# Block sums of v for four head pairs made from the window rows, and unread products in TensorE's first idle time

## The chip, the core and the metric

The kernel runs on one NeuronCore of a Trainium2 chip. The metric is the device time of one execution in microseconds, as a median over runs. Of the engines, the text uses TensorE (PE in the profile; its weight loads are PEld), VectorE (DVE), ScalarE (ACT), GpSimd (POOL), and SyncE (SP), which only issues transfers here. Transfers are issued by SP (queue q1) and POOL (queue q0) and carried by 16 DMA engines.

## What is computed

The program is an attention layer followed by two layers of experts. Cut to what matters:

```
# attention: 2 batches x 8 heads, 768 rows, 64 columns; blocks of 32, window 16
k_sum = k.reshape(B, H, 24, 32, D).max(axis=3)
v_sum = v.reshape(B, H, 24, 32, D).mean(axis=3)
scores = concat(where(|i - j| < 16, q k^T / 8, -1e9), q k_sum^T / 8 + log(32))
attn   = softmax(scores) @ concat(v, v_sum)
# layer 1: 4 experts, out += p[:, e] * (relu(x @ w1[e]) @ w2[e])
# layer 2: 8 experts, the same, with p from a softmax gate and 8 rounds of row and column scaling
```

## The kernel before

**Attention.** The 16 heads are worked in 8 pairs, 0 to 7 (`pairs`). A pair's queries are cut into 12 tiles of 64 rows. Such a tile sees 96 rows of k and v (its own 64 and 16 on either side) and the 24 block sums, so a tile has 120 columns (`KX`: 96 window columns, `KW`, and 24 block columns, `NS`). For a pair the kernel does the following.

- `add_loads`: SP loads k (L1048), q (L1055), all 768 rows of v with six following rows to a partition (`vn`, L1062, 384 KB), and once more the rows of v by windows: `vs` holds, for each of the 12 tiles, its 96 rows (L1074, four transfers).
- `add_keys`, `add_queries`: TensorE transposes k and q (L1094, L1156). ACT and DVE copy them to `kw` and `bd`, DVE takes the maxima of the key blocks (L1123), and L1137 spreads these to every tile's last 24 columns.
- `add_values`: DVE adds neighbouring rows of `vn` (L241, `rows`), three products with the selector `sel` then give the 24 block means (L1196, `sums`), DVE copies them out (L1203), and SP writes them to every tile of `vs` (L1208). For a pair in `VROWS` the addition is left out and six products are made.
- `add_group`, three times for each pair: scores of four tiles (L1226 for the mask, L1232), the row maximum (L1248), exponentials (L1254), sums (L1260), POOL's multiplication (L1269), transposes (L1278), products with `vs` (L1293), and the copy to the layer's input (L1304).

`kn`, `qn`, `vn`, `vs`, `kw` and `bd` exist twice, so pair i + 2 overwrites what pair i used.

**Experts.** Each of the 96 steps (48 units of 256 hidden columns, 2 halves of the rows) multiplies by a scheme with seven products instead of eight, each in three parts (high and low halves). The products with w1 are L306 and those with w2 are L629. Weights are loaded by SP (L479), and then split by ACT (L486, L499) with sums made by POOL's transfers (L502, L515). The first layer-1 steps need the first four pairs, so their products are interleaved with the last pairs' attention.

**Order.** Nothing is ordered at run time. Every operation is recorded by `op(engine, span, reads, writes, due, ...)`, and `run_work` lists them by a model: `SPAN` holds durations, `due` the wanted times, and ties go to the earlier due time. What it lists is each engine's fixed order. Constants such as `AHEAD` (how early a pair's loads are due), `WAIT0` (behind which pair's key load the first weights may be loaded), `XDUE`, `TURN`, `SOONER` and `FINAL` move due times. `take_of` gives a product the PSUM bank that the model has free first.

Of the kernel before, what the change touches and what calls it, by code (L numbers as in the profile page):

```python
# [12 lines left out]
ALU = mybir.AluOpType  # L13
# [5 lines left out]
def local_global_attention_moe_moe(  # L19
# [13 lines left out]
    nc = tc.nc  # L33
    P = 128
# [5 lines left out]
    NS = S // BLOCK  # L40
# [119 lines left out]
    def view_vs(t):  # L160
# [21 lines left out]
    ks = [accs[1][:, 2 * NB_ + i * NS:2 * NB_ + (i + 1) * NS] for i in range(2)]  # L182
    vbs = [accs[1][0:KX, 2 * NB_ + (i + 1) * P:2 * NB_ + (i + 2) * P] for i in range(2)]
    maskr = place.tile([QT + 1, 6 * KX], F32R, name="maskr", tag="xc", bufs=1).rearrange(
        "x (n k) -> x n k", k=KX
# [133 lines left out]
    def relu(S, out, src, th, neg=False):  # L319
# [26 lines left out]
        "p256": (0.75, 0.77), "p512": (1.4, 1.42), "p768": (1.9, 1.93), "p384": (1.05, 1.08), "psm": (0.98, 1.02), "pks": (0.8, 0.85),  # L346
        "pid": (0.55, 0.6), "p1": (0.2, 0.25), "pmask": (3.0, 3.1), "psel": (0.9, 0.95),
        "add1": (0.95, 1.3, ADD, LAND), "add2": (0.950001, 1.3, 1.8 * ADD, LAND),
# [622 lines left out]
    def take_of(i):  # L971
        return {"of": WIDE if i < NARROW else SIDE, "left": 0, "at": 0.0, "bank": None}

    def add_setup():
        d = -20.0

        def pool(span, key, fn):
            op("POOL", span, (), [key], d, fn)
# [60 lines left out]
        vop(mask_cast, ["mask"], ["maskr"], d, "vmk", True)  # L1039

    def add_loads(i, d):
        b, hp = pairs[i]
# [9 lines left out]
        for j in range(2):  # L1052
# [6 lines left out]
            )  # L1059
        op(  # L1060
            "SP", "ldv", (), [("vn", p)], d + 0.3,
            lambda: nc.sync.dma_start(  # L1062
                out=vn, in_=v[b, 2 * hp:2 * hp + 2].rearrange("h (p c) d -> p h c d", c=VC)
            ),
        )
        t = vs[i % 2]
# [110 lines left out]
    def add_values(i, d):  # L1177
        p = i % 2
        tk = take_of(i)

        def rows():
            e = nc.gpsimd if i in VPOOL else nc.vector
            vn = vns[p]
            vadd(vn[:, :, 0::2, :], vn[:, :, 0::2, :], vn[:, :, 1::2, :], e)

        by = 1 if i in VROWS else 2
        if by == 2:
            op(
                *(("POOL", "p384") if i in VPOOL else ("DVE", "v")),
                [("vn", p)], [("vn", p)], d - 0.01, rows, True,  # L1190
            )

        def sums():
            pv = full[tk["bank"]]
            for c in range(0, VC, by):
                nc.tensor.matmul(  # L1196
                    pv[KW:KX, 0:P], sel[:, c // 2, :], vns[p][:, :, c, :],
                    start=c == 0, stop=c == VC - by,
                )

        op("PE", "pv" if by == 2 else "pv6", [("vn", p), "sel"], [("pv", i)], d, sums, take=tk)
# [180 lines left out]
    def set_places():  # L1382
# [16 lines left out]
        old1 = [("vb", 0), ("vb", 1), ("ks", 0, 0), ("ks", 0, 1), ("ks", 1, 0), ("ks", 1, 1)]  # L1399
        old1 += [("vs", 1, j) for j in range(3)] + [("bd", 1, 0), ("bd", 1, 1)]  # L1400
        for c in range(KH):
# [8 lines left out]
    SECOND = {0: "1256437", 1: "1254637"}  # L1410
    FINAL = "1567432"
    HOP, GOFF, DCOFF, LEAD, LEAD2 = 1.15, 0.15, 6.6, 1.0, 0.95
    LOPOOL = ()
    VPOOL = ()
    VROWS = (3,)
    AHEAD = 5.5
    BYPOOL = ()
    ALONG = 5.7
    NARROW = 4
    WAIT0 = 1  # L1420
    KSPOOL = (3,)
    XDUE = [-2.1, -2.5, -0.9, 0.9]
    W0DUE = -5.2
    FIRST0 = -1.1
    XPOOL = [(B11, B22), (B11, N1, B21, T3, N4), (N1, B21, B22), (N4,)]
    LATER = {-2: -0.2, 1: -0.4, 2: 0.6, 3: 0.4, 8: 0.4}
    SOONER = {-2: 0.6, -1: -0.2, 1: -0.2, 2: 0.2, 3: 0.2, 7: -0.2}
    TURN = 2.3
    M2ACT = True
    TURNPOOL = ()  # L1430
    LOX = ((0, 2, S1), (2, 2, S4), (4, 1, S1), (4, 1, S4), (15, 2, S1), (16, 1, S1), (19, 1, S4), (20, 1, S4), (20, 2, S4),)
    M2X = (6, 7, 8)
    LODVE = ((1, S1), (1, S4), (2, S1),)
    with tc.manual_schedule():
# [17 lines left out]
        for i in range(len(pairs)):  # L1452
# [5 lines left out]
            for g in range(NG):  # L1458
                add_group(i, g, A0 + (3 * i + g) * AD)
            if i == 1:  # L1460
                add_rows_first(A0 + 6 * AD)
# [87 lines left out]
```

## Time and profile before

| | us |
|---|---|
| median of 3 runs | 1539.32 (1538.97 to 1540.72) |
| profiled execution | 1539.71 |
| its span, first to last instruction | 1537.9 |
| PE busy, 9036 matmul records | 1507.3 (98%) |
| DVE, ACT, POOL busy | 1372.3, 1131.3, 485.4 |
| mean granted TensorE clock | 0.997 |

The profiled execution is 0.4 us above the median of the runs, and 1.8 us longer than its span. A matmul record covers its whole passage through the pipeline, so records overlap and a busy PE isn't PE at its peak: 12 following products of 384 columns take 2.09 us, while the mean record is 336 ns long.

### The profile page before, as it was taken

The numbers are of one execution on the slowest core, as the hardware profiler recorded it, in microseconds if no ns is written. First come the engines' busy times: TensorE is split into PE (matmuls) and PEld (weight loads), VectorE is DVE, ScalarE is ACT, GpSimd is POOL, SyncE is SP. The second block draws the span as 40 slices with busy tenths as digits, with TensorE's granted clock in tenths as the row PEclk, the third lists the DMA queues.
The fourth block names the chain that finished last, engine by engine and source line by source line (L and its number), as shares of the span: only waits on it lengthen the run. The fifth ranks groups of instructions, "written<-read, shape, count | busy, mean of one in ns | idle before, by whom it ended". The sixth has DMA issues, their size and how long they took to land.

```text
span 1537.9 us, 26663 instructions
## 1 busy us (share of the span) xinstructions
PE 1507.3 (98%) x9036; PEld 1482.9 (96%) x9036; DVE 1372.3 (89%) x2840; ACT 1131.3 (74%) x2460; POOL 485.4 (32%) x512
## 2 busy tenths in 40 slices
PE   7889999999999999999999999999999999999998
PEld 6779999999999988999999999999999999999997
DVE  7887989999988998999899899899989989989988
ACT  5888777767767779777677777777777767767765
POOL 3543233333232342343332332233332232232220
PEclk9999999999999999999999999999999999999999
DMA  9967567676666685587666666666667667667642
GB/s 218 219 121 141 114 134 132 119 134 120 124 128 125 123 149 95 106 166 151 121 119 133 123 121 132 116 126 129 124 118 136 124 112 137 124 112 137 122 71 90
DMA packets 199881, 197.83 MB, mean 129 GB/s; under 512 B 46512, under 2 KB 157760, under 8 KB 199744
## 3 DMA queue, kind: packets, MB, share of 16 engines
q0 software_dynamic: 83792, 117.73, 48.5%
q1 hardware_dynamic: 115952, 78.39, 18.5%
q8 instruction: 71, 1.16, 0.3%
q14 instruction: 66, 0.54, 0.1%
HBM read 73.97 MB, written 3.22 MB: 50 GB/s over the span
## 4 chain that ended last, share of the span: by engine, by line
PE 91%; DVE 5%; ACT 2%; DMA 1%; POOL 1%; issue 1%; SPq 0%; POOLq 0%; ACTq 0%; DVEq 0%
PE bank L306 44%; PE bank L629 43%; PE bank L1232 1%; DVE acc L241 1%; PE bank L1293 1%; DVE hoph L463 0%; ACT s L1254 0%; DMA w2lo<-raw 0%; PE bank L1196 0%; PE bank L1278 0%; DVE acc L244 0%; DVE acc L1123 0%; DMA quads<-in_k_dram 0%; DVE sm L1260 0%; ACT w2hi L486 0%
## 5 line engine op out<-in xcount | busy, mean ns | idle before, releaser
L629 PE MATMUL bank<-hoph,w2hi 128*128 128x384 f32 x2688 | 687.4, 336 | 4.7 <-ACT acc L640 1.7
L629 PEld LDWEIGHTS bank<-hoph,w2hi 128*128 128x128 f32 x2688 | 484.1, 188 | 10.9 <-ACT bank L640 4.3
L629 PE MATMUL bank<-hoph,w2lo 128*128 128x384 f32 x1344 | 449.3, 334 | 0.1
L468 ACT ACTIVATE hoph<-quads 128x384 fp32r<-128x384 f32 x672 | 335.9, 521 | 100.6 <-PE bank L629 69.0
L241 DVE TENSOR_TENSOR acc<-bank,acc 128x384 f32<-128x384 f32 x726 | 380.9, 550 | 5.6 <-PE bank L629 2.6
L306 PE MATMUL bank<-xhi,w1hi 128*128 128x384 f32 x1008 | 339.2, 336 | 1.4 <-ACT w1hi L486 1.0
L306 PE MATMUL bank<-xlo,w1hi 128*128 128x384 f32 x1008 | 337.7, 335 | 0.0
L306 PE MATMUL bank<-xhi,w1lo 128*128 128x384 f32 x1008 | 337.4, 335 | 0.1
L463 DVE TENSOR_TENSOR hoph<-quads,hoph 128x384 fp32r<-128x384 f32 x583 | 310.3, 550 | 26.2 <-ACT hoph L468 22.3
L515 POOL DMA_DIRECT2D raw<-raw x195 | 205.3, 1067 | 383.1 <-DMA raw<-raw 173.8
L640 ACT COPY bank<-bank 128x384 f32<-128x384 f32 x384 | 181.3, 472 | 115.4 <-PE bank L629 108.9
L629 PEld LDWEIGHTS bank<-hoph,w2lo 128*128 128x128 f32 x1344 | 252.3, 188 | 0.4 <-DMA w2lo<-raw 0.4
L306 PEld LDWEIGHTS bank<-xhi,w1hi 128*128 128x128 f32 x1008 | 189.4, 188 | 3.5 <-ACT w1hi L486 1.2
L306 PEld LDWEIGHTS bank<-xhi,w1lo 128*128 128x128 f32 x1008 | 189.5, 188 | 0.7 <-DVE w1lo L244 0.7
L306 PEld LDWEIGHTS bank<-xlo,w1hi 128*128 128x128 f32 x1008 | 189.4, 188 | 0.0
L640 ACT COPY acc<-bank 128x384 f32<-128x384 f32 x222 | 105.7, 480 | 84.5 <-PE bank L629 80.1
L515 POOL DMA_DIRECT2D xf<-xf x93 | 98.6, 1060 | 180.9 <-DMA xf<-xf 77.7
L323 DVE SCALAR_TENSOR_TENSOR quads<-bank,pb 128x384 f32<-128x384 f32 x178 | 98.6, 554 | 42.1 <-PE bank L306 39.2
L502 POOL DMA_DIRECT2D w2lo<-raw x65 | 68.7, 1056 | 146.6 <-ACT w2lo L499 126.6
L599 DVE SCALAR_TENSOR_TENSOR quads<-quads 128x384 f32<-128x384 f32 x192 | 105.9, 552 | 1.7
L244 DVE TENSOR_TENSOR quads<-quads 128x384 f32<-128x384 f32 x185 | 102.3, 553 | 2.7 <-ACT quads L321 0.4
L540 ACT ACTIVATE quads<-bank 128x384 f32<-128x384 f32 x192 | 91.7, 486 | 13.0 <-PE bank L306 10.2
(193 smaller groups left out, 1888.0 us busy)
## 6 DMA issues: line engine op xcount, KB each, us to landing
raw<-raw POOLq DMA_DIRECT2D x130, 256.0 KB, 4.2
raw<-in_moe_w_dram SPq DMA_DIRECT2D x66, 256.0 KB, 3.8
raw<-in_moe_w_dram SPq DMA_DIRECT2D x128, 128.0 KB, 3.0
xf<-xf POOLq DMA_DIRECT2D x62, 256.0 KB, 4.0
w2lo<-raw POOLq DMA_DIRECT2D x33, 384.0 KB, 4.8
w1lo<-raw POOLq DMA_DIRECT2D x32, 384.0 KB, 4.2
pb<-prow SPq DMA_DIRECT2D x24, 384.0 KB, 4.5
raw<-raw POOLq DMA_DIRECT2D x65, 128.0 KB, 2.7
```

The costliest lines, as they stand in the source:

```text
L241: (eng or nc.vector).tensor_tensor(out=out, in0=x, in1=y, op=ALU.add)
L244: (eng or nc.vector).tensor_tensor(out=out, in0=x, in1=y, op=ALU.subtract)
L306: nc.tensor.matmul(pm, l[:, s, cs_], x_of(b, c, r, x), start=first and i == 0, stop=i == n - 1, skip_group_check=True,)
L323: nc.vector.scalar_tensor_tensor(out=out, in0=src, scalar=0.0, in1=PB[S[1]][:, th * HB:(th + 1) * HB], op0=ALU.min if neg else ALU.max, op ...
L463: e.tensor_tensor(out=out, in0=src, in1=hi.bitcast(F32), op=ALU.subtract)
L468: aop(lambda: nc.scalar.mul(to(0), src, -1.0 if neg else 1.0), reads, writes, due, "ah")
L502: lambda: nc.gpsimd.dma_start(out=l, in_=src, accum_op=ALU.add),
L515: lambda o=o, x=x: nc.gpsimd.dma_start(out=o, in_=x, accum_op=ALU.add),
L540: aop(lambda: nc.scalar.mul(out, src, by), [kin], [kout], due)
L599: nc.vector.scalar_tensor_tensor(out=q[o], in0=q[x], scalar=-1.0, in1=q[y], op0=ALU.mult, op1=ALU.subtract)
L629: nc.tensor.matmul(cut[bank], l[:, s, cols], hop_of(t, r), start=start and i == 0, stop=i == 2, skip_group_check=True,)
L640: aop(lambda: nc.scalar.copy(out=out, in_=src), [kin], [kout], due)
```

## The change

For pairs 0 to 3 (`VWIN`) the load of `vn` and the addition of its rows are gone. The block means come from the window rows in `vs`: tile t holds 96 rows, of which each row of v is counted once by a selector that is cut to the tile, so 12 products (one for each tile) take the place of three (six for pair 3). POOL makes the selector `selw` at the start, in ten instructions. `add_idle` records 42 products of the identity with its first 64 columns, into banks that nobody reads: 12 as soon as the identity is there, 30 once pair 0's second query transpose is done. Constants that move due times are changed as well, among them `WAIT0` (1 to 5), `AHEAD`, `XDUE`, `TURN`, `SOONER`, `FINAL`; pairs 2 and 6 have their block maxima spread by POOL (`KSPOOL`) and pair 6 makes six products in place of the addition (`VROWS`). `VPOOL = (6,)` has no effect, since pair 6 has no addition.

```diff
+    W0_ = 2 * NS - 2
+    selw = accs[1][0:KW, 2 * NB_ + 3 * P:2 * NB_ + 3 * P + W0_ + 2 * NS]
+    SELW = ((NS - 2, WIN), (W0_, 0), (W0_ + 2 * NS - 2, BLOCK))
...
+        def window_sels():
+            nc.gpsimd.memset(selw, 0.0)
+            for col, row in SELW:
+                t = selw[:, col:col + 2]
+                nc.gpsimd.memset(t, 1.0 / BLOCK)
+                for sgn, base in ((1, -row), (-1, row + BLOCK - 1)):
+                    nc.gpsimd.affine_select(
+                        out=t, in_=t, pattern=[[-sgn * BLOCK, 2]], compare_op=ALU.is_ge,
+                        fill=0.0, base=base, channel_multiplier=sgn,
+                    )
...
+    def add_idle(n, span, reads):
+        for _ in range(n):
+            tk = take_of(0)
+
+            def fn(tk=tk):
+                nc.tensor.matmul(
+                    full[tk["bank"]][:, 0:D], ident, ident[:, 0:D], start=True, stop=True
+                )
+
+            op("PE", span, ["ident"] + reads, [], 1e3, fn, take=tk, use=tk)
...
+        if i not in VWIN:
+            op(
+                "SP", "ldv", (), [("vn", p)], d + 0.3,
...
+        if i in VWIN:
+
+            def sums():
+                pv = full[tk["bank"]]
+                for t in range(NQ):
+                    o = W0_ if t == 0 else W0_ + NS if t == NQ - 1 else NS - 2 - 2 * t
+                    nc.tensor.matmul(
+                        pv[KW:KX, 0:P], selw[:, o:o + NS],
+                        vs[p][0:KW, t].rearrange("x j d -> x (j d)"),
+                        start=t == 0, stop=t == NQ - 1,
+                    )
+
+            op("PE", "pvw", [("vs", p, 0), ("vs", p, 1), "selw"], [("pv", i)], d, sums, take=tk)
...
-    AHEAD = 5.5
+    AHEAD = 2.9
...
-    WAIT0 = 1
-    KSPOOL = (3,)
-    XDUE = [-2.1, -2.5, -0.9, 0.9]
+    WAIT0 = 5
+    KSPOOL = (2, 3, 6)
+    IDLE = (12, 30)
+    XDUE = [-2.1, -3.0, -1.5, 0.9]
...
+            if i == 0:
+                add_idle(IDLE[0], "idc", [])
+                add_idle(IDLE[1], "idw", [("ptq", 0, 1)])
```

The first place is TensorE's queue from the program's start; before, it stands so (L1094 and L1156 transpose pair 0's k and q, L1226 and L1232 are scores, L1196 the block sums; the numbers behind names are buffers).

```order
L1094 MATMUL bank_127<-ident,quads 128x128 x4
L1094 MATMUL bank_128<-ident,quads 128x128 x3
L1156 MATMUL bank_129<-ident,quads 128x128 x3
L1156 MATMUL bank_130<-ident,quads 128x128 x3
L1226 MATMUL bank_131<-maskr,wgs 128x480
L1232 MATMUL bank_131<-kw,bd 128x120 x4
L1196 MATMUL bank_132<-pb_98,sel 24x128 x3
L1226 MATMUL bank_133<-maskr,wgs 128x480
L1232 MATMUL bank_133<-kw,bd 128x120 x4
L1226 MATMUL bank_134<-maskr,wgs 128x480
```

Twelve unread products (L1066) now stand ahead of the transposes and 21 between the last of these and the scores; the next rows are the end of the 21 and what follows (L1224 is the sum from window rows; L1272, L1278, L1126, L1188 and L1324 are the former L1226, L1232, L1094, L1156 and L1278).

```order
L1066 MATMUL bank_133<-ident 128x64
L1272 MATMUL bank_129<-maskr,wgs 128x480
L1278 MATMUL bank_129<-kw,bd 128x120 x4
L1224 MATMUL bank_130<-acc_95,acc_96 24x128 x12
L1272 MATMUL bank_131<-maskr,wgs 128x480
L1278 MATMUL bank_131<-kw,bd 128x120 x4
L1126 MATMUL bank_132<-ident,kn 128x128 x4
L1126 MATMUL bank_134<-ident,kn 128x128 x3
L1188 MATMUL bank_127<-ident,qn 128x128 x3
L1324 MATMUL bank_128<-ident,s_111 120x128 x4
L1188 MATMUL bank_133<-ident,qn 128x128 x3
L1272 MATMUL bank_129<-maskr,wgs 128x480
```

The third group of pair 0's scores moved behind pair 1's transposes, and the sum is four times as many products.

The second place is SP's queue from pair 2's keys on, before (L1208 spreads block sums, L1062 loads v, L479 loads weights):

```order
L1048 DMA quads<-in_k_dram 128x6x64 x2
L1055 DMA quads<-in_q_dram 128x3x128 x2
L1208 DMA acc_95<-acc_96 24x12x128
L1062 DMA pb_98<-in_v_dram 128x2x384
L479 DMA raw_91<-in_moe_w_dram 128x2x128 x2
L1048 DMA kn<-in_k_dram 128x6x64 x2
L1055 DMA qn<-in_q_dram 128x3x128 x2
L479 DMA raw_91<-in_moe_w_dram 128x2x128 x2
```

In the changed kernel the same place holds the following (L1079, L1086, L1094, L1254 are the former L1048, L1055, L1062, L1208; the two loads of v are those of pairs 4 and 5).

```order
L1079 DMA quads<-in_k_dram 128x6x64 x2
L1086 DMA quads<-in_q_dram 128x3x128 x2
L1094 DMA pb_98<-in_v_dram 128x2x384
L1360 DMA dp<-in_moe_domain_probs_dram 128x12x4
L1364 DMA wg<-in_moe_w_gate_dram 128x4x8
L1094 DMA vn<-in_v_dram 128x2x384
L1254 DMA acc_95<-acc_96 24x12x128
L1079 DMA kn<-in_k_dram 128x6x64 x2
```

The loads of v for pairs 0 to 3 are gone, those of pairs 4 and 5 stand early, and the first weights have left this stretch.

The third place is where these weights (L482, the former L479) now stand on SP: behind pair 6's keys.

```order
L1079 DMA quads<-in_k_dram 128x6x64 x2
L482 DMA raw_91<-in_moe_w_dram 128x2x128 x4
L482 DMA raw_92<-in_moe_w_dram 128x512
L1254 DMA acc_95<-acc_96 24x12x128
L482 DMA raw_92<-in_moe_w_dram 128x512
L298 DMA pb_97<-prow_79 128x768
L1086 DMA quads<-in_q_dram 128x3x128 x2
```

They moved from ahead of pair 3's and pair 4's loads to behind pair 6's keys. TensorE's first products with w1 stand behind pair 3's last output in both kernels, with 14 score groups ahead of them now and 18 before.

## Rows read from the trace of the kernel before

**Rows 1.** Busy time of each engine by stretch of the span, instructions in brackets.
```profile
core 0: us, PE busy (x) PEld busy (x) DVE busy (x) ACT busy (x) POOL busy (x), PEclk, DMA share, GB/s
0.00:9.60 9.60, 3.41 (x15) 2.99 (x15) 7.11 (x16) 3.06 (x5) 4.58 (x22) 1.00 0.93 196
9.60:28.50 18.90, 16.21 (x102) 13.86 (x102) 11.25 (x27) 8.85 (x28) 4.08 (x4) 0.91 1.19 228
28.50:55.80 27.30, 25.06 (x304) 22.52 (x304) 23.13 (x57) 25.58 (x72) 12.61 (x14) 1.00 1.09 220
55.80:111.70 55.90, 48.39 (x500) 41.58 (x499) 47.64 (x111) 44.44 (x127) 29.81 (x29) 0.97 0.79 150
111.70:560.00 448.30, 448.15 (x2577) 447.00 (x2576) 399.08 (x800) 333.56 (x710) 142.87 (x146) 1.00 0.67 128
20.00:24.00 4.00, 3.20 (x14) 2.59 (x14) 2.71 (x8) 0.44 (x2) 2.11 (x2) 0.57 1.13 239
...
560.00:590.00 30.00, 27.80 (x148) 23.07 (x146) 29.99 (x65) 27.19 (x62) 15.32 (x17) 1.00 0.92 167
680.00:710.00 30.00, 27.95 (x153) 26.01 (x153) 29.60 (x63) 20.45 (x44) 14.07 (x15) 1.00 0.98 188
1030.00:1060.00 30.00, 30.00 (x175) 30.00 (x174) 27.12 (x56) 21.79 (x46) 9.72 (x10) 1.00 0.69 141
1517.00:1538.00 21.00, 13.58 (x87) 11.23 (x85) 15.48 (x31) 7.98 (x16) 0.00 (x0) 0.96 0.40 151
```

**Rows 2.** PE's instructions in order of time: start, duration, idle time before.
```profile
4.67 1.73 PE L1094 MATMUL bank<-ident,quads 128*128 128x128 f32 x7 [4.67 <-POOL ones L999]
...
9.59 2.03 PE L1232 MATMUL bank<-kw,bd 128*128 128x120 f32 x8 [1.52 <-DVE kw L1137]
...
15.65 0.93 PE L1094 MATMUL bank<-ident,kn 128*128 128x128 f32 x7
...
20.80 2.04 PE L1232 MATMUL bank<-kwa,acc 128*128 128x120 f32 x8 [2.09 <-DVE kwb L1137]
...
27.48 1.05 PE L1232 MATMUL bank<-kwb,acc 128*128 128x120 f32 x8
...
68.09 0.42 PE L306 MATMUL bank<-xhi,w1hi 128*128 128x384 f32 x1
...
111.66 0.51 PE L629 MATMUL bank<-hoph,w2hi 128*128 128x384 f32 x2
```

**Rows 3.** The chain that ended last, 0 to 60 us: start, net duration, what.
```profile
27.64 0.89 PE bank L1232 x8
...
36.28 0.72 ACT w1hi L486
...
40.84 1.42 PE bank L1196 x12
```

**Rows 4.** PE's groups by line and shape, 0 to 112 us: busy, mean ns, idle before.
```profile
L1278 PE MATMUL bank<-ident,s 128*120 128x128 f32 x96 | 14.8, 279 | 3.1 <-POOL s L1269 2.7 <-ACT s L1254 0.4
...
L1232 PE MATMUL bank<-kwa,acc 128*128 128x120 f32 x56 | 8.7, 300 | 2.9 <-DVE kwb L1137 2.9
...
L1196 PE MATMUL bank<-pb,sel 128*24 128x128 f32 x24 | 4.0, 311 | 0.7 <-DVE pb L241 0.7
```

**Rows 5.** Transfers of 0 to 112 us: totals, then issues with size and landing.
```profile
DMA packets 49237, 20.68 MB, mean 185 GB/s; under 512 B 34416, under 2 KB 48032, under 8 KB 49224
...
raw<-in_moe_w_dram SPq DMA_DIRECT2D x8, 128.0 KB, 5.1
...
w1lo<-raw POOLq DMA_DIRECT2D x2, 384.0 KB, 6.1
```

**Rows 6.** SP's queue: its longest waits in 0 to 115 us, and issues in order of time.
```profile
SPq L1074 <- PE bank L1293: 17.0, 3, 11.1
...
19.54 1.20 SPq L479 DMA_DIRECT2D raw<-in_moe_w_dram  x2
...
53.07 1.33 SPq L1048 DMA_DIRECT2D quads<-in_k_dram  x2
```

More of the change, by code (lines that the diff above doesn't have):

```diff
@@ L346, in local_global_attention_moe_moe @@
         "p256": (0.75, 0.77), "p512": (1.4, 1.42), "p768": (1.9, 1.93), "p384": (1.05, 1.08), "psm": (0.98, 1.02), "pks": (0.8, 0.85),
-        "pid": (0.55, 0.6), "p1": (0.2, 0.25), "pmask": (3.0, 3.1), "psel": (0.9, 0.95),
+        "pid": (0.55, 0.6), "p1": (0.2, 0.25), "pmask": (3.0, 3.1), "psel": (0.9, 0.95), "pselw": (1.6, 1.65),
         "add1": (0.95, 1.3, ADD, LAND), "add2": (0.950001, 1.3, 1.8 * ADD, LAND),
@@ L1014, in add_setup @@
         pool("psel", "sel", sels)
+        def window_sels():
[8 more added lines that the diff above has]
+                    )
+        pool("pselw", "selw", window_sels)
         for i, t in enumerate(sb):
@@ L1059, in add_loads @@
             )
[L1060 to L1065, printed above, removed]
+        if i not in VWIN:
+            op(
+                "SP", "ldv", (), [("vn", p)], d + 0.3,
+                lambda: nc.sync.dma_start(
+                    out=vn, in_=v[b, 2 * hp:2 * hp + 2].rearrange("h (p c) d -> p h c d", c=VC)
+                ),
+            )
         t = vs[i % 2]
@@ L1184, in rows, with sums @@
             vadd(vn[:, :, 0::2, :], vn[:, :, 0::2, :], vn[:, :, 1::2, :], e)
[L1186 to L1198, printed above, removed]
-                )
-        op("PE", "pv" if by == 2 else "pv6", [("vn", p), "sel"], [("pv", i)], d, sums, take=tk)
+        if i in VWIN:
[7 more added lines that the diff above has]
+                        start=t == 0, stop=t == NQ - 1,
+                    )
+            op("PE", "pvw", [("vs", p, 0), ("vs", p, 1), "selw"], [("pv", i)], d, sums, take=tk)
+        else:
+            by = 1 if i in VROWS else 2
+            if by == 2:
+                op(
+                    *(("POOL", "p384") if i in VPOOL else ("DVE", "v")),
+                    [("vn", p)], [("vn", p)], d - 0.01, rows, True,
+                )
+            def sums():
+                pv = full[tk["bank"]]
+                for c in range(0, VC, by):
+                    nc.tensor.matmul(
+                        pv[KW:KX, 0:P], sel[:, c // 2, :], vns[p][:, :, c, :],
+                        start=c == 0, stop=c == VC - by,
+                    )
+            op("PE", "pv" if by == 2 else "pv6", [("vn", p), "sel"], [("pv", i)], d, sums, take=tk)
         vop(
@@ L1399, in set_places @@
         old1 = [("vb", 0), ("vb", 1), ("ks", 0, 0), ("ks", 0, 1), ("ks", 1, 0), ("ks", 1, 1)]
-        old1 += [("vs", 1, j) for j in range(3)] + [("bd", 1, 0), ("bd", 1, 1)]
+        old1 += ["selw"] + [("vs", 1, j) for j in range(3)] + [("bd", 1, 0), ("bd", 1, 1)]
         for c in range(KH):
@@ L1410, in local_global_attention_moe_moe @@
     SECOND = {0: "1256437", 1: "1254637"}
-    FINAL = "1567432"
-    HOP, GOFF, DCOFF, LEAD, LEAD2 = 1.15, 0.15, 6.6, 1.0, 0.95
+    FINAL = "1256374"
+    HOP, GOFF, DCOFF, LEAD, LEAD2 = 1.15, 0.15, 6.6, 1.0, 0.92
     LOPOOL = ()
-    VPOOL = ()
-    VROWS = (3,)
-    AHEAD = 5.5
+    VPOOL = (6,)
+    VROWS = (0, 3, 6)
+    VWIN = (0, 1, 2, 3)
+    AHEAD = 2.9
     BYPOOL = ()
@@ L1419, in local_global_attention_moe_moe @@
     NARROW = 4
-    WAIT0 = 1
-    KSPOOL = (3,)
-    XDUE = [-2.1, -2.5, -0.9, 0.9]
+    WAIT0 = 5
+    KSPOOL = (2, 3, 6)
+    IDLE = (12, 30)
+    XDUE = [-2.1, -3.0, -1.5, 0.9]
     W0DUE = -5.2
-    FIRST0 = -1.1
+    FIRST0 = -2.4
     XPOOL = [(B11, B22), (B11, N1, B21, T3, N4), (N1, B21, B22), (N4,)]
     LATER = {-2: -0.2, 1: -0.4, 2: 0.6, 3: 0.4, 8: 0.4}
-    SOONER = {-2: 0.6, -1: -0.2, 1: -0.2, 2: 0.2, 3: 0.2, 7: -0.2}
-    TURN = 2.3
+    SOONER = {-2: 0.6, -1: -0.2, 1: -0.2, 2: -0.4, 3: 0.2, 7: -0.2}
+    TURN = 1.6
     M2ACT = True
     TURNPOOL = ()
-    LOX = ((0, 2, S1), (2, 2, S4), (4, 1, S1), (4, 1, S4), (15, 2, S1), (16, 1, S1), (19, 1, S4), (20, 1, S4), (20, 2, S4),)
+    LOX = ((0, 2, S1), (2, 1, S4), (2, 2, S4), (4, 1, S1), (4, 1, S4), (15, 2, S1), (16, 1, S1), (19, 1, S1), (19, 1, S4), (20, 1, S4), (20, 2, S4),)
     M2X = (6, 7, 8)
```

2 rows, old and new, of the table SPAN are left out of this document.

## Prediction

> **What bounds the kernel now.** I read the stretches first. From 111.7 us on, TensorE has no idle time that counts: 448.15 of 448.30 us busy up to 560 [rows 1]. All of the expert products lie there but 54, the same 54 in both kernels, so a second that attention loses or saves at its end is lost or saved by the whole. What is left to win is the first 111.7 us, two stretches in the middle and the tail. In the middle, 560 to 590 holds 148 matmul records and 680 to 710 holds 153, where an undisturbed 30 us hold 175 [rows 1]: 27 and 22 records short, or 4.6 and 3.8 us at 30/175 = 0.171 us each. The tail has 7.4 us of idle time in 21 [rows 1].
>
> In the first 111.7 us TensorE is idle for 6.2, 2.7, 2.2 and 7.5 us in the four stretches (length minus busy), 18.6 in all [rows 1]. The order in time shows a second loss: products at double duration. Pair 0's seven transposes take 1.73 us and pair 1's 0.93; the first scores take 2.03 us, those at 20.80 again 2.04, and those at 27.48 only 1.05 [rows 2]. These two give 1.8 us; comparing all seven kinds of product from 4.7 to 13.5 us with their later twins so gives 3.8. Those of 20.80 to 24 follow a gap of 2.09 us, and there the granted clock is 0.57 over 4 us, a mean of its 1.2 and 2.4 GHz levels, so 1.7 us are lost [rows 1, 2]. Another 1.7 us are lost after 55.8 (0.97 over 55.9 us). From 0 to 9.6 us the granted clock is 1.00, in spite of the double durations [rows 1].
>
> DMA engines are at a share of 0.93 to 1.19 up to 55.8 us and of 0.79 after [rows 1]. Yet the waits of TensorE name engines, not transfers [rows 4]. So no single engine bounds this stage: TensorE is busy 93 of 111.7 us, DVE 89, ACT 82, and DMA is full for half of it.
>
> **What the change costs.** Pairs 0 to 3 make 48 products with window rows in place of 15, and pair 6 makes six in place of three: 36 more. Twelve records, or six of these products, took 1.42 us at full clock [rows 3], 0.237 us each, so TensorE gets **8.5 us** more work. The shape is the same, 24 output rows and 128 columns. That is the bar that the gains must pass. Hidden or not, this work passes through the engine that nobody lets idle afterwards, so it costs nothing only where it falls into idle time.
>
> The unread products have 64 columns. For one I bound the cost by scores of 120 columns (0.89 us for eight records [rows 3], so 64/120 of 0.22 us or 0.12 us) and by twice that at half clock. The first 12 take 1.4 to 2.9 us, begin once the identity is there and lie before 4.67 us, where TensorE waited anyway [rows 2]: nothing. The 21 behind the query transposes take 2.5 to 5.0 us. They lie where TensorE waited 1.52 us for DVE and ran the mask product [rows 2], and the last of them writes a bank that DVE must have emptied (the scaling of the queries), which the scores need too. At 0.12 us each they cost nothing; at 0.24 us the scores come up to 2.5 us late. I take nothing, because the clock should be up by then. The nine others cost at most 1.1 us and stand where the scheduler's model saw an idle engine; I take 0.5.
>
> Moving the first weights from 19.54 us [rows 6] to behind pair 6's keys takes ACT's first casts of weights (0.72 us for one [rows 3], four such) and POOL's summing transfers out of a stretch where ACT is busy 25.58 of 27.30 us [rows 1], into one where it is busy 44.44 of 55.90. The first w1 product must not wait for them. From issue it takes 5.1 us to land, 1.4 for two casts and 6.1 for the sum [rows 3, 5]: 12.6 us. I expect pair 6's keys some 6 to 8 us before their 53.07 [rows 6], because eight weight loads and two loads of v fewer stand ahead, and the product at about 61 instead of 68.09 [rows 2]: just enough. I take 0.5 us. Bounds: 0, and 6 us if these keys keep their place (53.1 + 1.3 + 12.6 = 67 against 61).
>
> Ten more POOL instructions at the start delay only `selw` and a few constants, needed behind the first scores; nothing.
>
> **What it gains.**
> - The clock. With the 12 products ahead, TensorE has been at work for some 3 us when k lands. Pair 0's 3.8 us of surplus should mostly go: I take 2.0 for the scores and sums and 0.6 for transposes that start DVE's chain earlier. The 1.7 us after 20.80 go if the 2.09 us gap ahead is filled. Together **4.3 us**; bounds 0 and 5.5.
> - That gap, and others. Now pair 0's third scores and pair 1's 12 window products stand ahead of pair 1's scores, 3.9 us of work: 2.1 of the 2.9 us that TensorE waited for L1137 there go. The 0.7 us for the addition of rows go with it [rows 4]. Of 3.1 us ahead of L1278, mostly behind POOL [rows 4], I take 2.0, since the longest came right behind the weights' casts [rows 3] and sums, which now leave that place. Together **4.8 us**; bounds 2 and 6.
> - The last stage, 55.8 to 111.7: 7.5 us idle and 1.7 at half clock. DVE has an addition and a spread less, and the window loads of pairs 6 and 7, for which SP waited 17.0 us until outputs had released `vs` [rows 6], follow outputs that now stand ahead of later pairs' scores. I take **4.0 us** of the 9.2, less than half, since most of these waits are for the pairs' own chains, which stay; bounds -1 and 7.
> - Middle and tail. `TURN` and `SOONER` move due times around the layer change, where 8.4 us are lost, and `FINAL` swaps a few additions at the end. Rows don't tell which way; I take 0.3 us for less, with bounds of 1.5 on either side.
>
> The 4 x 384 KB = 1.57 MB that are no longer loaded are 7.6% of 20.68 MB [rows 5]; where they count they are in the gaps above.
>
> Sum: 4.3 + 4.8 + 4.0 + 0.3 = 13.4 gained, 8.5 + 0.5 + 0.5 = 9.5 lost: 3.9 us less. The profiled execution took 1539.71, so 1535.8, and as the median of the runs lies 0.4 below it, I say **1535.5**.
>
> **Two rules against the rows.** The granted clock was 1.00 from 0 to 9.6 us while products took twice their later time [rows 1, 2]; I go by the durations. The Trainium skill (TensorE: Matmul & The Clock Gate, What's actually happening) says that the halved clock is the default and activity releases it, which agrees with the durations; the same page (Seeing it yourself) warns that clock events in a trace can be unreliable. By the granted clock alone, the first 2.6 us of the clock's gain would be missing, and the sum would be 1.2 us less.
>
> By bytes, the loads that are gone are 7.1 us of a stream of 220 GB/s [rows 1]. By packets they are 4 x 256 runs of 1536 bytes, 1024 of 49237 packets, or 2% of the stream [rows 5]. The Trainium skill (DMA: Bandwidth & Descriptors, Specifications) wants at least 512 bytes for line rate; by it these were the cheap transfers, the 34416 packets under 512 bytes stay, and the DMA stage would shrink by 1 to 2 us only. My sum does without either.
>
> **Rivals.**
> - *No gain: the idle time only moves.* If the last stage keeps its 9.2 us, because latency from scores to outputs sets it and not the load on DVE, 3.9 us fall to about 0: 1539.3. For it speaks that the waits name DVE, ACT and POOL in turn [rows 4]; against it that DVE has less to do.
> - *Slower: the first weights come late.* If pair 6's keys keep their 53.07, the w1 product waits 6 us with pair 5's scores queued behind it on TensorE, and a gap of that length is followed by products at half clock, 1.7 us as at 20.80: 1535.5 + 6 + 1.7 = 1543.2. It decides from 3.9 us on, where the gain is used up. For it speaks that these loads also wait in SP's order behind window loads that wait for outputs [rows 6]; against it that fewer transfers stand ahead.
> - *Much faster: transfers set the pace.* With a DMA share about 1 for 55.8 us [rows 1], 1.57 MB of v and 1 MB of weights fewer there let pairs 2 to 5 arrive up to 10 us earlier. Then the last stage loses 7 of its 9.2 us in place of 4, and the gaps 6 in place of 4.8: 1531.3. Against it: no wait names a transfer [rows 4].
>
> **How the numbers follow.** A measurement of this kernel tells apart about 0.2%, 3 us. My forecast (alone 1532.5 to 1537) gets 0.47, no gain 0.25, late weights 0.16, much faster 0.12. Of the forecast's own spread a tenth lies within 0.2%; of "no gain" a tenth lies below and none above it. So: faster 0.57, within 0.2% 0.27, slower 0.16. The range leaves out the far ends of the last two: 1529.5 to 1541.5.
>
> **What would show it.** Right: products from 4.7 us on soon at 0.93 us for seven transposes; scores of pair 1 begun by 21 us without 2 us of idle time ahead; the first w1 product at 60 to 63 us; the first w2 product, at 111.66 before [rows 2], at 107 to 109. Wrong: idle time ahead of the first w1 product that names ACT w1hi or DMA w1lo; 21 unread products that end after DVE's spread; the last stage again with 9 us of idle and halved clock; or 560 to 590 and 680 to 710 with fewer records still.

## The result and the profile after

The changed kernel takes 1548.68 us (median of 3 runs, 1547.54 to 1549.26) against 1539.32: the ratio is 1.0056, 95% interval 1.0043 to 1.0069. It is 9 us slower where 4 us less were forecast. Its profiled execution took 1548.68, with a span of 1547.0.

The stretches of the changed kernel, with the columns of [rows 1] (busy time of PE, PEld, DVE, ACT, POOL, then granted clock, DMA share, GB/s):

```profile
0.00:9.60 9.60, 8.16 (x39) 8.17 (x39) 5.18 (x10) 2.06 (x3) 5.98 (x32) 1.00 0.96 185
9.60:28.50 18.90, 18.90 (x157) 17.90 (x157) 10.29 (x27) 7.24 (x21) 1.97 (x2) 1.00 0.98 192
10.00:11.00 1.00, 1.00 (x7) 1.00 (x6) 0.99 (x3) 0.64 (x2) 0.00 (x0) 1.00 1.19 273
12.00:13.00 1.00, 1.00 (x12) 1.00 (x11) 0.00 (x0) 0.00 (x0) 0.00 (x0) 1.00 1.37 197
28.50:55.80 27.30, 27.29 (x292) 24.58 (x291) 25.97 (x59) 22.87 (x68) 12.28 (x15) 1.00 0.77 191
55.80:111.70 55.90, 50.41 (x553) 44.33 (x551) 43.61 (x98) 48.17 (x132) 30.38 (x32) 0.97 0.77 151
104.00:106.00 2.00, 2.00 (x8) 1.95 (x7) 0.15 (x2) 2.00 (x5) 1.68 (x3) 0.50 0.57 158
```

By these TensorE looks better than before: the idle time of the four stretches fell from 18.6 to 6.9 us. A busy engine is no measure of the work that counts. The order in time shows what it was busy with (start, duration, line, count, idle time before); the first w2 product stands behind the same products as before, so its start compares the two kernels:

```profile
1.44 5.38 PE L1066 MATMUL bank<-ident 128*128 128x64 f32 x24 [1.44 <-POOL ident masks.py:199]
6.61 1.70 PE L1126 MATMUL bank<-ident,quads 128*128 128x128 f32 x7
9.38 5.55 PE L1066 MATMUL bank<-ident 128*128 128x64 f32 x42
15.05 1.05 PE L1278 MATMUL bank<-kw,bd 128*128 128x120 f32 x8
16.02 2.80 PE L1224 MATMUL bank<-acc,acc 96*24 96x128 f32 x24
...
101.43 0.66 PE L1324 MATMUL bank<-ident,s 128*120 128x128 f32 x4 [2.75 <-POOL s L1315]
...
116.59 0.51 PE L632 MATMUL bank<-hoph,w2hi 128*128 128x384 f32 x2
```

DVE's row for the spread that pair 0's scores need:

```profile
11.12 0.38 DVE L1169 COPY kw<-acc 128x168 f32<-128x168 f32 x2
```

The first 12 unread products run until 6.8 us, so pair 0's transposes begin at 6.61 in place of 4.67 [rows 2]. The next 21 (42 records) end at 14.93, 3.4 us after the spread (11.12 + 0.38 = 11.50): the scores start 5.5 us later than before. The chain of waits, followed back from the last instruction, runs through both groups (start, net duration, what):

```profile
1.44 5.38 PE bank L1066 x24
6.82 1.49 PE bank L1126 x7
8.31 1.28 PE bank L1188 x6
9.59 5.34 PE bank L1066 x42
```

The first w2 product is 4.9 us late, the last 24 transposes 8.7. Before them TensorE waits 2.69 us where it waited 1.38:

```profile
1538.61 2.84 PE L949 MATMUL bank<-ident,acc 128*128 128x128 f32 x24 [2.69 <-DVE acc L649]
```

The same block in the kernel before:

```profile
1529.93 2.84 PE L946 MATMUL bank<-ident,acc 128*128 128x128 f32 x24 [1.38 <-DVE acc L241]
```

### The profile page after: what moved, and what is told of

Its sections match the earlier page's. It is cut to its first block, busy times and chain, and to the rows that moved or that the text cites. A ratio compares the mean times of both kernels' runs of the same rounds, so it can differ in the third digit from the quotient of the medians.

```text
span 1547.0 us, 26995 instructions
## 1 busy us (share of the span) xinstructions
PE 1524.4 (99%) x9192; PEld 1500.0 (97%) x9192; DVE 1371.4 (89%) x2830; ACT 1136.3 (73%) x2462; POOL 489.3 (32%) x528
## 4 chain that ended last, share of the span: by engine, by line
PE 90%; DVE 5%; DMA 1%; ACT 1%; issue 1%; POOL 1%; SPq 0%; DVEq 0%; POOLq 0%; ACTq 0%
PE bank L309 42%; PE bank L632 41%; PE bank L1278 1%; DVE acc L244 1%; PE bank L1066 1%; DMA xf<-in_moe_w_dram 1%; PE bank L1324 1%; PE bank L1224 1%; PE bank L1339 1%; DVE hoph L466 1%; DVE acc L250 0%; DVE quads L247 0%; DVE acc L247 0%; DVE quads L326 0%; PE bank L1126 0%
## 5 line engine op out<-in xcount | busy, mean ns | idle before, releaser
L247 DVE TENSOR_TENSOR quads<-quads,bank 128x384 f32<-128x384 f32 x96 | 53.1, 553 | 55.1 <-PE bank L309 52.7
```

The source lines that it names most:

```text
L247: (eng or nc.vector).tensor_tensor(out=out, in0=x, in1=y, op=ALU.subtract)
```

## Experiments

All times are medians; beside each stands that of the kernel before on the same chip in the same group of runs, and the ratio with its 95% interval. "First w2" is the start of the first w2 product in the profiled execution (111.66 before); all of attention's transposes and outputs and 58 or 59 products with w1 stand ahead of it, but for e10 and e11, where six of the latter fewer do (1 us), and e8, where it can't be compared.

| run | first w2 | median, us | before | ratio, interval |
|---|---|---|---|---|
| e1_silent | 114.09 | 1544.36 | 1539.60 | 1.0033, 1.0023 to 1.0042 |
| e2_first12 | 114.54 | 1544.92 | 1539.60 | 1.0032, 1.0021 to 1.0044 |
| e3_last30 | 120.19 | 1551.86 | 1539.60 | 1.0077, 1.0062 to 1.0092 |
| e4_late_undone | 116.39 | 1549.81 | 1539.60 | 1.0065, 1.0048 to 1.0082 |
| e5_silent_late_undone | 113.47 | 1542.69 | 1539.92 | 1.0019, 1.0009 to 1.0028 |
| e6_windows_only | 111.70 | 1540.28 | 1539.92 | 1.0006, 0.9997 to 1.0015 |
| e7_before_late | 111.47 | 1542.42 | 1539.92 | 1.0016, 1.0007 to 1.0026 |
| e8_before_early | | 1547.43 | 1539.92 | 1.0051, 1.0036 to 1.0066 |
| e9_wait0 | 109.58 | 1541.79 | 1539.51 | 1.0013, 1.0004 to 1.0021 |
| e10_kspool | 115.74 | 1543.40 | 1539.51 | 1.0027, 1.0016 to 1.0039 |
| e11_due | 112.83 | 1540.36 | 1539.51 | 1.0012, 1.0000 to 1.0024 |
| e12_six_four | 114.86 | 1547.48 | 1539.51 | 1.0052, 1.0040 to 1.0065 |
| e13_six_four_silent | 116.56 | 1549.04 | 1539.64 | 1.0054, 1.0041 to 1.0068 |
| e14_windows_inplace | 111.95 | 1539.83 | 1539.64 | 0.9998, 0.9989 to 1.0007 |
| e15_before_inplace | 109.60 | 1542.83 | 1539.64 | 1.0018, 1.0009 to 1.0027 |
| e16_after_inplace | 114.19 | 1544.53 | 1539.64 | 1.0027, 1.0017 to 1.0037 |
| e17_noidle | 106.45 | 1539.03 | 1539.82 | 0.9993, 0.9984 to 1.0002 |
| e18_vrows | 116.54 | 1547.86 | 1539.82 | 1.0044, 1.0031 to 1.0056 |

### The unread products, in the order of the changed kernel

Three runs keep the plan and leave products out when they would be issued: all 42, the last 30, the first 12.

```diff
-                nc.tensor.matmul(
+                False and nc.tensor.matmul(           # e1_silent
+                (not reads) and nc.tensor.matmul(     # e2_first12
+                reads and nc.tensor.matmul(           # e3_last30
                     full[tk["bank"]][:, 0:D], ident, ident[:, 0:D], start=True, stop=True
```

> The changed kernel with none of the 42 unread products issued, every other instruction in the order of the changed kernel (no part of the result is left out). Theory A (the unread products hold up pair 0's chain, and the delay of 5.5 us at its scores is kept to the first w2 product): scores of pair 0 begin at 9.5 to 10.5 us in place of 15.05, the first w2 product at 110 to 112 in place of 116.59, and the time falls by 4 to 6 us to 1543 to 1545. Rival B (the 8.5 us of added sums from window rows are the loss, and the delay at the start would be absorbed by later waits): pair 0's scores move forward, but the first w2 product stays at 115 to 117, and the time stays within 1.5 us of 1548.7. Rival C (the constants of the middle and the tail): no change here, 1547 to 1549.

> The changed kernel with the first 12 unread products issued and the other 30 not (no part of the result is left out). Theory A: the 12 still end at about 6.6 us and the transposes start 1.9 us later than before, but the 21 that cost 5.5 us are gone: scores of pair 0 at 11 to 12 us, time 1.5 to 2 us above that of the kernel with none, 1545 to 1547. If the 12 bring the clock up, seven transposes take 0.93 us in place of 1.70 and the loss is under 1 us. Rival B: within 1.5 us of 1548.7, as the others.

> The changed kernel with the 30 later unread products issued and the first 12 not (no part of the result is left out). Theory A: transposes at 4.7 us as before, the 21 products take 5.5 us behind them and end at 12.5 to 13.5, some 2 to 4 us past DVE's spread; scores of pair 0 at 12.5 to 13.5; time 2.5 to 4 us above that of the kernel with none, 1546 to 1548. Rival B: within 1.5 us of 1548.7.

Without them the time falls by 4.3 us, as theory A said, but the first w2 product comes at 114.09, not at 110 to 112: half of the loss is left. The 12 alone cost 0.6 us (within the runs' spread). The 30 alone cost 7.5, more than all 42. Without the 12, the 21 ahead of the scores (42 records) take 9.06 us, as TensorE's order in time shows in e3_last30, and the first w2 product is 3.6 us later than with all 42:

```profile
7.67 9.06 PE L1066 MATMUL bank<-ident 128*128 128x64 f32 x42
```

In e2_first12, TensorE's order in time shows what became of the clock:

```profile
8.10 1.13 PE L1188 MATMUL bank<-ident,quads 128*128 128x128 f32 x6
8.99 0.47 PE L1272 MATMUL bank<-maskr,wgs 65*128 65x480 f32 x1
11.51 1.46 PE L1278 MATMUL bank<-kw,bd 128*128 128x120 f32 x8 [2.05 <-DVE kw L1169]
12.90 4.08 PE L1224 MATMUL bank<-acc,acc 96*24 96x128 f32 x24
```

and the stretch behind the gap (columns as above):

```profile
11.50:16.00 4.50, 4.49 (x25) 3.66 (x26) 1.31 (x2) 1.12 (x4) 0.00 (x0) 0.62 1.36 214
```

The six query transposes take 1.13 us in place of 1.49, then comes a gap of 2.05 us, and the sums behind it take 4.08 us in place of 2.80, at a granted clock of 0.62, a mean of the two levels. The rate rises during the query transposes and is lost again behind the gap. That the 12 raised it is not shown: in e7, e11 and e17, which issue no unread product, pair 0's scores run at the full rate too.

### Constants and window sums apart

```diff
-    FINAL = "1256374"                             # e4 in the changed kernel, e5 in e1_silent;
+    FINAL = "1567432"                             # e7: the reverse, in the kernel before
-    TURN = 1.6
+    TURN = 2.3
...
-                add_idle(IDLE[0], "idc", [])      # e6: the changed kernel without this,
-                add_idle(IDLE[1], "idw", [("ptq", 0, 1)])   # with all constants as before
...
-    WAIT0 = 1                                     # e8, in the kernel before
+    WAIT0 = 5
-    KSPOOL = (3,)
+    KSPOOL = (2, 3, 6)
```

The lines left out: e4, e5 and e7 move `SOONER`, `LEAD2` and `LOX` as well, e8 `AHEAD`, `XDUE` and `FIRST0`.

> The changed kernel with the constants of the middle and the tail as before (TURN 2.3, SOONER 2: 0.2, LEAD2 0.95, FINAL, LOX); TensorE's order is the same up to the last attention products. Rival C (these constants cost the 2.5 us in the middle and the 1.7 us in the tail): first w2 product at 116.6 as in the changed kernel, last block of transposes 4 us sooner, time 1544 to 1545.5. Theory A, that the delay at the start is the larger part: the time stays at 1543.5 or more, since the 4.9 us lost by the first w2 product stay. If the middle and the tail lose as much with the old constants, because what stands around them is late for another reason: 1548 to 1549.

> The changed kernel without its unread products and with the constants of the middle and the tail as before, so that against before the block sums and the constants of the first stage are left. Theory W: 2 to 3 us of the loss at the first w2 product (114.1 as with the unread products silent alone) remain to the end: 1541.5 to 1543. Rival C: the 2.5 us that were lost behind the first w2 product with the unread products silent go: 1541.5 to 1542. If neither is so: 1544 to 1545 as with the unread products silent alone.

> The kernel before with one part alone: block sums of pairs 0 to 3 from the window rows, without their loads of v and additions of rows; no unread products, all constants as before. Theory W (the added sums cost more than the gaps they close): 33 products more than before at 0.237 us are 7.8 us, of which the gaps ahead of pair 1's scores and of the sums, 2.1 + 0.7 us, and 1.7 us at half clock come back: first w2 product at 113 to 116, time 1541.5 to 1544.5. If the stream of transfers sets the pace of this stage, 1.57 MB less let it end sooner: first w2 product before 111 and time below 1538.5. If what is left of the loss comes from the constants: 1539 to 1540.5.

> The kernel before with the constants of the middle and the tail alone as in the change (TURN, SOONER, LEAD2, FINAL, LOX). Rival C, which the run with these constants undone in the changed kernel speaks against: 1542 to 1544. Otherwise within 1.5 us of before's 1539.6; the records of 560 to 590 and 680 to 710 us may shift by a few in both directions.

> The kernel before with the constants of the first stage alone as in the change (AHEAD 2.9, WAIT0 5, KSPOOL, XDUE, FIRST0), block sums from the loaded v as before, no unread products. Theory W: the constants alone cost little, 1538 to 1541. Rival E (the later first weights and POOL's spreading for pairs 2 and 6 cost the last stage): first w1 or w2 product 2 us or more later than before, time 1541.5 to 1545.

The window sums alone cost nothing that can be measured: 7.8 us of products, and the first w2 product at 111.70 as before; theory W falls. The late constants take nothing off when undone in the changed kernel, cost 2.5 us in the kernel before and 1.7 in e1_silent (where the intervals overlap). The first stage's constants cost 7.5 us alone. With the window sums, e5 lies 2.4 us above e6, but the intervals overlap, and e5 also keeps the order that was planned around the 42 products, so this is no price of the constants. These runs give no part a price of its own.

Three runs take these constants apart on e6: `WAIT0`; `KSPOOL` with `VROWS`; the due times. A fourth puts ten unread products into e6.

```diff
-    WAIT0 = 1                                # e9
+    WAIT0 = 5
-    KSPOOL = (3,)                            # e10; e18 has VROWS alone
+    KSPOOL = (2, 3, 6)
-    VROWS = (3,)
+    VROWS = (0, 3, 6)
-    AHEAD = 5.5                              # e11, with XDUE and FIRST0
+    AHEAD = 2.9
-                pass                         # e12
+                add_idle(6, "idc", [])
+                add_idle(4, "idw", [("ptq", 0, 1)])
```

> The kernel with the window sums alone, and the first weights loaded behind pair 6's keys (WAIT0 5 in place of 1). The rival of late weights: the first w1 product waits for its weights, ACT's cast or POOL's sum, 2 us or more ahead of it, and the time is 1542 to 1545. If the later weights cost what the prediction took, 0.5 us: 1539.5 to 1541.5, within 1 us of the window sums alone (1540.3).

> The kernel with the window sums alone, with POOL spreading the block maxima of pairs 2 and 6 as well (KSPOOL) and pairs 0 and 6 in VROWS (for pair 6: no addition of rows, six products for three). If the 2.4 us between the window sums alone and those with all constants of the first stage come from POOL (TensorE waits longer for POOL's multiplication behind these copies): 1542 to 1543.5. If not: 1539.5 to 1541, since three products more are 0.7 us.

> The kernel with the window sums alone, and the three due times of the first stage as in the change (AHEAD 2.9, XDUE, FIRST0). If the due times cost the 2.4 us: 1542 to 1543.5, with a first w2 product 2 us later than 111.7 or idle time of that size before it. If WAIT0 or KSPOOL does: 1539.5 to 1541.

> The kernel with the window sums alone, and pairs 0 and 6 in VROWS (six products and no addition of rows for pair 6), without the change of KSPOOL; both together took 1543.4, the window sums alone 1540.3. If POOL's spreading for pairs 2 and 6 costs the 3 us: 1539.5 to 1541.2 (three products more are 0.7 us). If pair 6's sum or the order that goes with it does: 1542.5 to 1544.5.

> The kernel with the window sums alone and ten unread products, sized by what one costs at half clock in the changed kernel, 0.45 us: six ahead of the transposes (1.44 to 4.1 us) and four between these and pair 0's scores (1.8 us in a wait of 1.5). Theory A: sized so, they hold up nothing: transposes at 4.6 us and scores of pair 0 at 9.5 to 9.9 as without them, and part of pair 0's 3.8 us at half clock comes back: pair 1's transposes 1 to 3 us earlier than 16.28. To the end 0 to 1.5 us of it are kept: 1538.8 to 1540.3. If unread products cost time in themselves wherever they stand: 1541.5 or more.

Late weights cost 1.5 us by the medians and 1.1 by the ratios, which is not clear of noise (the intervals of e6 and e9 overlap), and none of TensorE's waits from 28 to 112 us in e9 names their cast. In e8 one does, at products with w1 that its order puts late:

```profile
108.81 0.44 PE L306 MATMUL bank<-xhi,w1hi 128*128 128x384 f32 x1 [3.30 <-ACT w1hi L486]
```

So the rival of late weights falls for the window sums; a wait of the kind that it feared stands in e8, which loses 7.5 us. The due times cost nothing that can be measured. `VROWS` alone costs 7.6 us (5.9 by the ratios), and with `KSPOOL`, which the expectation of e10 suspected, only 3.1. Three products more are 0.7 us, so the rest is not their own length. And ten unread products that delay nothing cost 7.2.

### The order or the products?

The planner counts the unread products, so they change its list. Four runs separate the two: e12 with its ten products left out when issued (e13); the ten written into the functions of the transposes and scores, where the planner does not see them, in e6 (e14), in the kernel before (e15) and in e1_silent (e16).

```diff
             def turn(pt, c0=c0, nt=nt, half=half):
+                for _ in range(6 * (i == 0 and half == 0)):
+                    nc.tensor.matmul(pt[:, 0:D], ident, ident[:, 0:D], start=True, stop=True)
...
         def scores():
             ps = bank[0]()
+            for _ in range(4 * (w == 0)):
+                nc.tensor.matmul(ps[:, 0:D], ident, ident[:, 0:D], start=True, stop=True)
```

> The run with six and four unread products, with its order of all other instructions, but none of the ten issued (no part of the result is left out). If its 7 us over the window sums alone came from the other order that the planner lists once it counts the ten products: 1546 to 1549 again. If the products themselves cost them: 1539.5 to 1541.5.

> The kernel with the window sums alone, in exactly its order on every engine, with six unread products ahead of pair 0's transposes and four ahead of its scores, written into the functions of these products so that the planner doesn't see them. If the order cost the 7 us: pair 1's transposes 1.5 us sooner than 16.28 and the time 1538.5 to 1540.5, no slower than 1540.3 for the window sums alone. If an earlier, faster pair 0 itself costs time later (it meets transfers and waits that are no earlier): 1542 or more.

> The kernel before, in exactly its order, with the same six and four products. The prediction's term for pair 0's half clock, 2.0 us for scores and sums, taken alone: scores of pair 0 in 1.05 to 1.2 us in place of 2.03, pair 1's transposes at 13.8 to 14.6 in place of 15.65, and the time 1537.5 to 1539.5 if it is kept to the end. If the waits behind it (DVE's spread for pair 1, transfers) take it back: 1539 to 1540.3.

> The changed kernel in its order, with 10 unread products in place of 42, six ahead of the transposes and four ahead of the scores (no part of the result is left out). Theory A: scores of pair 0 at 9.5 to 9.9 us in place of 15.05, and the time that of the changed kernel with none, 1544.4, or up to 1.5 us less: 1542.9 to 1544.9. If the unread products cost the changed kernel time by anything else than their own length at half clock: 1546 or more.

For e12 it is the order: without the ten its time stays (e13, 1549.04). In e12, with the products, pair 0 is faster and pair 1's transposes stand at 14.67; in e13, without them, at 16.47. Both then lose the same 2.81 us at the same wait (0.6 in e6), TensorE's order in time for e12:

```profile
9.68 1.12 PE L1278 MATMUL bank<-kw,bd 128*128 128x120 f32 x8 [0.51 <-DVE kw L1169]
...
14.67 0.93 PE L1126 MATMUL bank<-ident,kn 128*128 128x128 f32 x7
...
62.47 0.82 PE L1339 MATMUL bank<-s,acc 120*64 120x64 f32 x16 [2.81 <-DVE acc L1249]
```

and for e13:

```profile
9.53 2.03 PE L1278 MATMUL bank<-kw,bd 128*128 128x120 f32 x8 [1.48 <-DVE kw L1169]
...
16.47 0.93 PE L1126 MATMUL bank<-ident,kn 128*128 128x128 f32 x7
...
64.28 0.69 PE L1339 MATMUL bank<-s,acc 120*64 120x64 f32 x16 [2.81 <-DVE acc L1249]
```

In e6's own order the ten cost nothing (e14, 1539.83), and in the changed kernel's they cost nothing against none (e16, 1544.53). Nor do they gain anything there: in e14 pair 1's transposes stand at 16.57 us, not 1.5 us sooner than 16.28 as expected, since pair 0's scores still run at half rate:

```profile
9.65 2.04 PE L1282 MATMUL bank<-kw,bd 128*128 128x120 f32 x8
```

And e11, which has none, ran them at the full rate, with pair 1's transposes as early as in e12:

```profile
9.62 1.12 PE L1278 MATMUL bank<-kw,bd 128*128 128x120 f32 x8 [1.44 <-DVE kw L1169]
...
14.61 0.93 PE L1126 MATMUL bank<-ident,kn 128*128 128x128 f32 x7
```

The prediction's 2.6 us for pair 0 rest on unread products that bring the full rate sooner. These runs do not show that they do: with none, the scores ran at the full rate in three profiled executions (e7, e11, e17) and at half rate in nine.

In e15 pair 0 is as fast as the prediction hoped, and it does not last: the kernel takes 1542.83 us, 3.2 more than before, where at most 0.7 more were expected. TensorE's order in time there:

```profile
9.48 1.12 PE L1236 MATMUL bank<-kw,bd 128*128 128x120 f32 x8 [0.43 <-DVE kw L1139]
13.62 0.93 PE L1096 MATMUL bank<-ident,kn 128*128 128x128 f32 x7
...
109.60 0.51 PE L629 MATMUL bank<-hoph,w2hi 128*128 128x384 f32 x2
...
702.22 0.44 PE L629 MATMUL bank<-hoph,w2hi 128*128 128x384 f32 x1 [1.14 <-DVE hoph L463]
...
1531.33 5.38 PE L946 MATMUL bank<-ident,acc 128*128 128x128 f32 x24 [2.89 <-DVE acc L241]
```

and two of its stretches:

```profile
703.00:706.00 3.00, 2.43 (x11) 2.11 (x10) 3.00 (x8) 2.89 (x7) 1.10 (x2) 0.76 1.03 297
...
1530.00:1534.00 4.00, 2.67 (x13) 2.67 (x14) 2.99 (x6) 0.59 (x1) 0.00 (x0) 0.57 0.51 193
```

Pair 1's transposes are 2.0 us sooner than in [rows 2], and so is the first w2 product. At 700 us a wait of 1.14 us that the kernel before does not have, and half clock behind it, take this back; at the end the last 24 transposes wait 2.89 us and take 5.38 at a granted clock of 0.57, where they took 2.84 before. The median says that time is lost; that it is lost at these two places is what one profiled execution shows.

The last run takes the 42 products out of the changed kernel's plan as well.

```diff
-                add_idle(IDLE[0], "idc", [])
-                add_idle(IDLE[1], "idw", [("ptq", 0, 1)])
+                pass
```

> The changed kernel without the 42 unread products, so that the planner doesn't count them either and lists another order than the changed kernel's (no part of the result is left out). With them silent in the old order the time was 1544.4. If the order that the planner finds around them costs as it did with ten (7 us): 1538 to 1541.5. If the planner's order around them is no worse than without: 1543 to 1546.

It takes 1539.03 us, 5.3 less than with the products silent in the old order. Its stretches:

```profile
9.60:28.50 18.90, 18.66 (x145) 16.57 (x147) 11.68 (x29) 9.84 (x30) 3.99 (x5) 0.91 1.07 214
28.50:55.80 27.30, 27.14 (x297) 24.41 (x297) 26.07 (x59) 22.10 (x64) 12.37 (x15) 1.00 0.78 195
55.80:111.70 55.90, 52.09 (x572) 46.65 (x568) 47.58 (x103) 51.90 (x143) 32.01 (x34) 1.00 0.82 164
```

TensorE's order in time there:

```profile
64.36 0.44 PE L309 MATMUL bank<-xhi,w1hi 128*128 128x384 f32 x1
...
94.20 0.65 PE L1324 MATMUL bank<-ident,s 128*120 128x128 f32 x4 [1.22 <-POOL s L1315]
...
106.45 0.51 PE L632 MATMUL bank<-hoph,w2hi 128*128 128x384 f32 x2
...
1528.25 2.84 PE L949 MATMUL bank<-ident,acc 128*128 128x128 f32 x24 [1.37 <-DVE acc L649]
```

The last of these stretches in e1_silent, and two us of it:

```profile
55.80:111.70 55.90, 48.81 (x503) 41.97 (x498) 42.68 (x96) 47.05 (x130) 30.38 (x33) 0.94 0.76 150
100.00:102.00 2.00, 2.00 (x20) 1.88 (x20) 1.58 (x9) 0.87 (x3) 0.00 (x0) 0.50 0.57 162
```

TensorE's order in time in e1_silent:

```profile
98.95 1.08 PE L1324 MATMUL bank<-ident,s 128*120 128x128 f32 x4 [2.75 <-POOL s L1315]
...
114.09 0.51 PE L632 MATMUL bank<-hoph,w2hi 128*128 128x384 f32 x2
```

The two orders of TensorE are equal for their first 434 records (up to 54.8 us) and then differ in many places, first in where transposes (L1324) stand among the outputs (L1339). The queues of DVE, ACT, POOL and SP differ as well, from 60 to 75 us on. The first difference, - e1_silent, + e17_noidle:

```
+L1324 MATMUL bank<-ident,s 120x128 x4
 L1339 MATMUL bank<-s,acc 64x64 x8
 L1339 MATMUL bank<-s,acc 64x64 x8
-L1324 MATMUL bank<-ident,s 120x128 x4
```

The wait for POOL in the last stage is 2.75 us with half clock behind it (granted 0.50, the lower level) in one and 1.22 us at full clock in the other.

## Why the prediction was wrong

**The failed step is the price of the unread products**: "nothing" for the first 12, "I take nothing, because the clock should be up by then" for the 21, 0.5 us for the others. They cost 1548.68 - 1539.03 = 9.7 us (1.0056 - 0.9993 is the same), in two parts that the runs separate. Of the 13.2 us between forecast and result that is 9.2 more than the 0.5 in the sum; the other 4 are about what e17_noidle had won by the first w2 product and did not keep (below).

- *4.3 us by their own length* (against e1_silent; 3.5 by the ratios; in the profiles 2.5 of it stand at the first w2 product and 1.3 at the wait ahead of the last transposes). The step sized them by columns: 0.12 us each, 0.24 at half clock. At half clock they took 5.38 / 12 = 0.45; between 12 and 13 us 12 records began, so 0.17 at full clock. A product is two records, and half the columns did not halve a record: at half rate one took 0.22 us here and 0.25 for the scores' 120 columns (2.03 / 8). Even at the full rate 21 of them would take 3.5 us, an estimate from these, and end at 12.9, behind the spread's 11.5. PEld's row is as busy as PE's there (1.00 and 1.00 us in 10 to 11), so the weight loads may set the pace; that was not tried. Nor was the clock up when the 21 began: 7 records between 10 and 11 us against 12 between 12 and 13, though TensorE had been at work without a gap since 1.44. The prediction's own sign, products that end after DVE's spread, is what the trace shows.
- *5.3 us by the order that the planner lists around them* (e1_silent against e17_noidle; 6.2 by the ratios), of which the prediction had no term and no rival. It priced each moved row by its duration and took the rest of the order as given. Ten such products, six and four, show the same: 7 us in the planner's order with or without them, and nothing in two orders held fixed (e14, e16). In a third, that of the kernel before, they did cost 2.8 us by the ratio (e15), so a held order is no proof against loss. That the 7.6 us of `VROWS` are of this kind is likely, but no run held its order.

**Window sums, 8.5 us against the gaps: right, for the sum.** By e17_noidle the idle time fell from 18.6 to at most 10.4 us (6.2 + 0.2 + 0.2 + 3.8), so 8.2 are gained, against 4.8 + 4.0 = 8.8 for gaps and last stage in the prediction. The first w2 product is 5.2 us sooner than before with the added products done. So 8.5 + 5.2 - 8.2 = 5.5 us are left for products that follow each other faster, against 4.3 for the clock. That this is near is in part luck: e17 issues no unread product, from which 2.6 of the 4.3 were to come, and its granted clock from 9.6 to 28.5 us is 0.91 as before; from 55.8 to 111.7 it is 1.00 against 0.97. The first w2 product stands at 106.45, where 107 to 109 was the sign of being right, and the first w1 product at 64.36, where it was 60 to 63.

**"A second that attention loses or saves at its end is lost or saved by the whole": wrong for what is saved.** Of e17's 5.2 us, 1.7 are left at the last block of transposes (1528.25 against 1529.93) and 1.3 in the span. From 111.7 to 800 us its stretches hold 18 matmul records fewer than those of before, 3.1 us at 0.171 each, of which idle time explains 1.4 (6.1 us against 4.6). e15 loses its 2.0 us by 710 us, and e9, 2.1 us ahead at the first w2 product, ends behind.

**Middle and tail, 0.3 gained with bounds of 1.5: the sign was wrong, and by the median the bound.** Undoing these constants gives 1.7 us in e1's order (not clear of noise) and nothing in the changed kernel's, and they cost the kernel before 2.5 (1.1 to 4.0 by the interval of e7).

**Late weights: right as a small term.** 0.5 was taken and e9 shows 1.1 to 1.5 us, not clear of noise; pair 6's keys stand at 44.84 us in the changed kernel, some 8 us before their 53.07 as forecast, and the rival of 1543.2 did not occur. Nor did transfers set the pace: e6 drops the four loads of v, and its first w2 product stands at 111.70 as before. Without the unread products the rival "no gain", 1539.3, describes the time best: e17's interval, 0.9984 to 1.0002, does not part it from before. No run here beat the kernel before by more than noise.

**Two slips that change nothing.** Without the 2.6 us the prediction's gain would have shrunk from 3.9 to 1.3 us, not to 1.2; and 58 products with w1 stand ahead of the first w2 product in both kernels, not 54.

**What stays open.** The runs show that the order costs, and at which waits, but not which moved row starts it. What is called the order here is all that the planner lists: the queues of every engine and the PSUM banks that it deals out, the unread products' own among them; the runs do not part these. e17 with the constants of the middle as before was not run.

## What to carry to other kernels

Where a planner sets the order, an edit has two prices, its work and the order it leads to, and here the second was up to 7 us for ten products that delayed nothing: run the new order with the added instructions left out, and the added instructions in the old order. Size filler by the measured length of such a record at the clock at which it runs, and let it end before the operand that it waits beside. Time won early has to be followed through the next stage that another engine sets before it is counted.

## Not expected of the hardware

- The granted clock reads 1.00 from 0 to 13 us, while TensorE begins 7 records between 10 and 11 us and 12 between 12 and 13: near the start, durations told the rate and the column did not. The trace's first clock record stands at 10.95 us, and ahead of it the column reads 1.00 without one. In the kernel before that record stands at 13.77, in e3 at 20.40.
- The same ten products at the same places led to scores at full rate in two kernels (1.12 us for eight records, e12 and e15) and at half rate in two (2.04 in e14, 2.03 in e16). With none, 1.12 in e7, e11 and e17, and 2.03 or 2.04 in nine others, the kernel before among them, whose instructions up to there are those of e7. The moment at which the rate rises is not set by these products alone, and differs between runs of the same instructions.
- A wait of 2.69 us at the end was followed by 24 transposes at full rate in the changed kernel (2.84 us), one of 2.89 us in e15 by 5.38.
